# The first FFT of a Fourier filter and feed-forward kernel in four quadrants of 32 partitions

## The chip, the cores and the metric

The kernel runs on one core of one Trainium2 chip. The metric is the time of one execution on the device in microseconds. A core has TensorE (PE, with its weight loads shown apart as PEld), VectorE (DVE), ScalarE (ACT), GpSimd (POOL), SyncE (SP, which here only issues transfers) and 16 DMA engines. Operands lie in SBUF, and TensorE writes its results to PSUM.

## The reference

```
X = rfft(x, axis=1)                 # x: 8 x 3008 x 256, float32
y = irfft(X * (filt_r + 1j*filt_i)) # filters: 1505 x 256, one per frequency and channel
h = maximum(y @ w_in, 0)            # y as 24064 tokens of 256; w_in: 256 x 2048
out = (h * h) @ w_out               # w_out: 2048 x 256
```

All inputs and the output are float32 in HBM. Both kernels compute in float16 with float32 sums in PSUM.

## The kernel before

**The FFT.** A length of 3008 is split into 64 x 47, and each stage is a matmul with constant cosine and sine matrices. Stage A (`unit_a`, L333; for the first batch `chunk_a0`, L366) takes the 47-point transforms. Stage B (`unit_b`, L411) takes the 64-point transforms of each of 24 classes `c` of frequencies, multiplies with the filter on DVE (L425) and leaves the products in float16. A product has two versions `v`, one with the real and one with the imaginary part of the filter. Stage P (`unit_p0`, L438, for batch 0; `unit_p`, L455, for the others) is the inverse 64-point transform, evicted by ACT into `ze` (L450) and written to a DRAM scratch `dZ`. `read_z` (L476) reads it back in another order into `zt`, and stage Y (`unit_y`, L484) is the inverse 47-point transform, whose result `yt` is the input of the feed-forward part. Batches 1 to 7 go through DRAM between A and B as well (`write_u`, L326, `dU`, `read_u`, L404). Batch 0 stays on the chip there: its A gives the transposed `uT`, and `turn_u` (L388) turns it back by matmuls with the identity, evicted at L400 and L402.

**The filter.** B's products need it as `sF`: rows of both signs of a frequency on 128 partitions, by class. `load_f` (L234) loads it as float32 with 3008 numbers a partition, `tensor_copy` casts it, and `place_f` (L269) moves each row to its partition by matmuls with the 0/1 matrices `sPF` (L284 and L287, 108 in all), evicted with the sign of its half at L295. Stage P of batch 0 takes the imaginary version with `sSPx`, a copy of the constant `sSP` with its halves exchanged (L773, L774).

**The feed-forward part** works on 47 groups of 512 tokens, 8 slots a group (loop at L809). In each slot `ffn_g1` (L512) computes two tiles of 128 hidden units into one of two `psH` buffers (2 PSUM banks each) and ACT takes the relu into float16 (L532). DVE squares (`ffn_sq`, L534). One group later `products` (L632) computes the second matmul in seven products of sums of quarters, for which `make_t` (L586, slots 8 to 11) and `sums` (L602) prepare operands on DVE.

**The order of the work.** The prologue, about 50 us, is written out by hand from L735 on: `warm` matmuls (26, L264), the casts of x (`cast_wide`, L221), A, `turn_u`, `place_f`, then B of two class pairs, a placement and P in a loop, then `read_z`, A of batch 1, 13 `fill` matmuls (L798) and the first four Y units (L801). Then the slot loop runs, into which `fft_plan` (L669) places the stages of batches 1 to 7 and the rest of Y of batch 0 by due times in slots: for example, B of batch 1 from slot 12 on, Y(0, n) for n of 4 to 7 in slots 4 to 7, n of 8 to 11 in slots 10 to 13, with the zt for these read by `read_z(0, 2)`, the last line of the prologue. Each engine executes its instructions in the order of the program and waits where an operand or a buffer isn't ready. SP issues nearly all transfers, in its own order; POOL issues the float32-to-float16 loads `load_x` and `load_wout` (L320).

**Buffers.** [...] two `psH` tiles of two banks, `psF` and `psO` tiles. `bank_pair` hands the prologue these in turn.

Of the kernel before, what the change touches and what calls it, by code (L numbers as in the profile page):

```python
# [22 lines left out]
QF = 3008  # L23
PQ = ((0, 0), (0, 1), (0, 2), (1, 2), (1, 3), (1, 0))


def _build_consts():
# [28 lines left out]
    freq[0, 32] = N // 2  # L56
# [6 lines left out]
    for c in range(NC):  # L63
        for f in range(64):
# [10 lines left out]
            if c == 0 and f == 32:  # L75
                SB[:, :, 1, c, :, f] = 0.0
# [18 lines left out]
    PF = np.zeros((128, 6, 2, 2, 32))  # L95
    for w, (s, q) in enumerate(PQ):
        for j in range(32):
            PF[4 * j + q, w, :, s, j] = 1.0

# [7 lines left out]
    return f16(C0, 128), f16(PF, 128), f16(SB, 128), f16(SP, 128)  # L107
# [3 lines left out]
def kernel(  # L111
# [19 lines left out]
    C0_np, PF_np, SB_np, SP_np = _build_consts()  # L131
    dPF = nc.inline_tensor(PF_np, name="cPF")
# [13 lines left out]
    p_y = ctx.enter_context(tc.tile_pool(name="p_y", bufs=2))  # L146
# [58 lines left out]
    sPF = p_out.tile([128, 6, 128], F16, tag="ost", name="sPF")  # L205
# [3 lines left out]
    def load_wide(k):  # L209

        v0 = xrows[0:2048, :].rearrange("(p m) d -> p m d", m=16)
        v1 = xrows[2048:3072, :].rearrange("(p m) d -> p m d", m=8)
        pool, tag = (p_x32, "x32") if k < 2 else (p_h2, "h2")
        t = pool.tile([128, 8, D], F32, tag=tag, name=f"xw_{k}")
        nc.sync.dma_start(out=t, in_=(v0[:, 0:8, :], v1, v0[:, 8:16, :])[k])
        xw32[k] = t
# [4 lines left out]
    def cast_wide(k, *engs):  # L221
        t = p_x16.tile([128, 8, D], F16, tag="x16", name=f"xw16_{k}")
        for i in range(2):
            m = slice(4 * i, 4 * i + 4)
            cast(engs[i], t[:, m, :], xw32[k][:, m, :])
        xw16[k] = t

    for k in range(3):
        load_wide(k)


    f32s = []

    def load_f(im):  # L234
        filt = filt_i if im else filt_r
        t = p_y.tile([128, QF], F32, tag="yt", name=f"f32_{im}")
        nc.sync.dma_start(out=t, in_=filt[0:1504, :].rearrange("a d -> (a d)")
                          .rearrange("(p e) -> p e", e=QF))
        f32s.append(t)

    load_f(0)
    nc.sync.dma_start(out=sPF, in_=dPF.ap().rearrange("p (w q) -> p w q", q=128))
    load_f(1)
    nc.sync.dma_start(out=sC1, in_=dC0.ap()[:, 704:896])
    nyq = p_out.tile([128, 2, D], F32, tag="ost", name="nyq")
    nc.gpsimd.memset(nyq, 0.0)
    for im, filt in enumerate((filt_r, filt_i)):
        nc.gpsimd.dma_start(out=nyq[0:1, im, :], in_=filt[1504:1505, :])
    sSB = const.tile([128, NC, 128], F16, name="sSB")
    sSP = const.tile([128, NC, 128], F16, name="sSP")  # L250
    sign = const.tile([128, 1], F32, name="sign")
    nc.vector.memset(sign[0:64], 1.0)
    nc.vector.memset(sign[64:128], -1.0)


# [8 lines left out]
    for _ in range(26):  # L264
        nc.tensor.matmul(ps, zero, sF[:, 0, 0:2, :], start=True, stop=True)  # L265

    f16s = []

    def place_f(im, k, *engs, rotate=False):  # L269

        if rotate:
            banks, groups = bank_pair(f"psf_{im}_{k}")
        else:
            t = psH(f"psf_{im}_{k}")
            banks, groups = [t[:, 0, :], t[:, 1, :]], [(t, 0)]
        for i in range(4):
            c = 4 * k + i
            e0, e1 = D * c, D * (47 - c)
            cuts = [0] + [d for d in range(1, D)
                          if (e0 + d) % QF == 0 or (c and (e1 + d) % QF == 0)] + [D]  # L280
            for d0, d1 in zip(cuts, cuts[1:]):
                o = banks[i // 2][:, (i % 2) * D + d0:(i % 2) * D + d1]
                q, a = divmod(e0 + d0, QF)
                nc.tensor.matmul(o, sPF[:, PQ.index((0, q)), :], f16s[0][:, im, a:a + d1 - d0],  # L284
                                 start=True, stop=False)
                q, a = divmod(e1 + d0, QF) if c else (0, QF + d0)
                nc.tensor.matmul(o, sPF[:, PQ.index((1, q)), :], f16s[0][:, im, a:a + d1 - d0],  # L287
                                 start=False, stop=True)
        for t, i in groups:
            n = t.shape[1]  # L290
            eng = engs[i % len(engs)]
            dst = sF[:, im, 4 * k + 2 * i:4 * k + 2 * i + 2 * n, :]
            src = t.rearrange("p t (a d) -> p (t a) d", d=D)
            if eng is nc.scalar:
                eng.activation(out=dst, in_=src, func=AF.Copy, scale=sign[:, 0:1] if im else 1.0)  # L295
            elif im:
                eng.tensor_scalar_mul(out=dst, in0=src, scalar1=sign[:, 0:1])
            else:
                eng.tensor_copy(out=dst, in_=src)
# [4 lines left out]
    def load_win():  # L304

        for k, c, n, pool, tag in ((0, 0, 768, p_ze, "ze"), (0, 768, 768, p_ze, "ze"),
# [26 lines left out]
    def unit_a(b, c):  # L333
# [29 lines left out]
        if b == 1:  # L363
            write_u(b, c)

    def chunk_a0(c):  # L366

        for k in range(2):
            banks, groups = bank_pair(f"psA_0_{c}_{k}")
# [410 lines left out]
    for k in range(7):  # L780
# [5 lines left out]
        if k > 0:  # L786
            unit_p0(k - 1)
# [72 lines left out]
```

## Time and profile before

| | |
|---|---|
| median of 3 runs | 760.74 us (760.02 to 760.77) |
| the profiled execution | 757.66 us |
| its span, from first to last instruction | 755.9 us |
| TensorE clock granted | 1.00 |
| PE busy | 741.9 us, 98% |
| DVE busy | 655.4 us, 87% |
| ACT busy | 564.2 us, 75% |
| POOL busy | 193.9 us, 26% |
| HBM traffic | 57.97 MB read, 48.23 MB written, 141 GB/s over the span |

A line of the chain of waits gives start, length, engine, the name of the result, the line of the kernel and a count. A line of the groups gives line, engine, operation, result <- operands, shapes and count, then busy us and mean ns of one, then the engine's idle time ahead of the group with what ended it. The prologue in the trace: the first cast of x starts at 6.32 us, the first turn_u matmul at 17.80, the last `ze` copy of batch 0 ends at 42.26, the first Y matmul starts at 48.76, the first L528 matmul of the loop at 50.21.

### The profile page before, as it was taken

The numbers are of one execution on the slowest core, as the hardware profiler recorded it, in microseconds if no ns is written. First come the engines' busy times: TensorE is split into PE (matmuls) and PEld (weight loads), VectorE is DVE, ScalarE is ACT, GpSimd is POOL, SyncE is SP. The second block draws the span as 40 slices with busy tenths as digits, with TensorE's granted clock in tenths as the row PEclk, the third lists the DMA queues.
The fourth block names the chain that finished last, engine by engine and source line by source line (L and its number), as shares of the span: only waits on it lengthen the run. The fifth ranks groups of instructions, "written<-read, shape, count | busy, mean of one in ns | idle before, by whom it ended". The sixth has DMA issues, their size and how long they took to land.

```text
span 755.9 us, 20010 instructions
## 1 busy us (share of the span) xinstructions
PE 741.9 (98%) x8419; PEld 542.8 (72%) x8419; DVE 655.4 (87%) x730; ACT 564.2 (75%) x803; POOL 193.9 (26%) x267
## 2 busy tenths in 40 slices
PE   8988999999999999999999999999999999999998
PEld 5845766777777777877778777787678777777776
DVE  5859998899899898989979998899989989888783
ACT  2967788778878777787777778777777777777773
POOL 3811750244222321232303224033311222000000
PEclk9999999999999999999999999999999999999999
DMA  9994898666785566756586646764547333321011
GB/s 364 298 221 147 144 185 224 174 115 121 165 220 121 97 130 161 194 104 133 107 216 127 131 102 131 229 126 101 115 108 207 80 78 92 99 85 43 30 57 57
DMA packets 103026, 106.51 MB, mean 141 GB/s; under 512 B 10144, under 2 KB 93472, under 8 KB 101400
## 3 DMA queue, kind: packets, MB, share of 16 engines
q1 hardware_dynamic: 83496, 81.99, 35.7%
q0 software_dynamic: 19296, 23.05, 22.1%
q8 instruction: 66, 1.08, 0.6%
q14 instruction: 24, 0.20, 0.1%
q10 hardware_dynamic: 144, 0.18, 0.1%
HBM read 57.97 MB, written 48.23 MB: 141 GB/s over the span
## 4 chain that ended last, share of the span: by engine, by line
PE 90%; DVE 5%; ACT 2%; DMA 1%; issue 1%; ACTq 0%; DVEq 0%
PE psH L528 40%; PE psX L643 21%; PE psY L643 16%; PE psY L498 3%; PE psB L417 2%; PE psP L462 2%; PE psA L348 2%; DVE prod L425 2%; PE warm L265 1%; PE psO L548 1%; ACT h L532 1%; DVE h L539 1%; PE psf L284 1%; PE psf L287 1%; DMA prod<-prod 1%
## 5 line engine op out<-in xcount | busy, mean ns | idle before, releaser
L532 ACT ACTIVATE h<-psH 128x1024 f16<-128x1024 f32 x376 | 385.3, 1026 | 160.2 <-PE psH L528 159.2
L528 PE MATMUL psH<-yt,sWin 128*128 128x512 f16 (+7 forms) x1728 | 386.8, 351 | 1.2 <-ACT h L532 0.4
L539 DVE TENSOR_TENSOR h<-h 128x2048 f16<-128x2048 f16 (+1 forms) x192 | 229.8, 1197 | 45.5 <-ACT h L532 45.1
L432 POOL DMA_DIRECT2D prod<-prod x168 | 138.8, 967 | 428.5 <-DVE prod L425 426.1
L528 PEld LDWEIGHTS <-sWin 128*128 128x128 f16 x1728 | 149.1, 98 | 90.5 <-issue 3.0
L643 PEld LDWEIGHTS <-sum 128*128 128x128 f16 x2944 | 181.4, 98 | 26.2 <-issue 6.3
L643 PEld LDWEIGHTS <-h 128*128 128x128 f16 x2208 | 135.6, 98 | 24.5 <-issue 5.3
L425 DVE TENSOR_TENSOR prod<-psB,sF 128x1024 f16<-128x1024 f32 x84 | 102.3, 1219 | 11.9 <-PE psB L417 11.8
L643 PE MATMUL psX<-sT,sum 128*128 128x128 f16 x1472 | 104.7, 219 | 0.0
L643 PE MATMUL psY<-sT,sum 128*128 128x128 f16 x736 | 71.2, 219 | 0.0
L643 PE MATMUL psY<-sWout,sum 128*128 128x128 f16 x736 | 56.0, 219 | 1.4 <-DVE bot L658 1.4
L617 DVE TENSOR_TENSOR sum<-sum,h 128x2048 f16<-128x2048 f16 x46 | 56.1, 1220 | 0.8
L643 PE MATMUL psY<-sWout,h 128*128 128x128 f16 x736 | 56.2, 219 | 0.0
L643 PE MATMUL psX<-sT,h 128*128 128x128 f16 x736 | 56.1, 219 | 0.0
L620 DVE TENSOR_TENSOR sum<-h 128x2048 f16<-128x2048 f16 x46 | 56.0, 1217 | 0.0
L623 DVE TENSOR_TENSOR sum<-h,sum 128x2048 f16<-128x2048 f16 x46 | 55.9, 1216 | 0.0
L195 POOL DMA_DIRECT2D x<-in_x_dram x64 | 55.8, 1045 | 0.5 <-PE psA L348 0.5
L614 DVE TENSOR_TENSOR sum<-h 128x2048 f16<-128x2048 f16 x46 | 55.9, 1215 | 0.0
L464 ACT CAST ze<-psP 128x512 f16<-128x512 f32 x84 | 49.2, 585 | 1.2 <-PE psP L462 1.1
L643 PE MATMUL psX<-sWout,h 128*128 128x128 f16 x736 | 48.7, 219 | 0.0
L507 DVE CAST yt<-psY 128x376 f16<-128x376 f32 x62 | 33.7, 543 | 14.3 <-PE psY L498 14.1
L498 PE MATMUL psY<-sC,zt 112*128 112x94 f16 x512 | 42.3, 204 | 1.3 <-DMA zt<-dZ 0.9
(78 smaller groups left out, 571.3 us busy)
## 6 DMA issues: line engine op xcount, KB each, us to landing
zt<-dZ SPq DMA_DIRECT2D x64, 192.0 KB
dU<-u SPq DMA_DIRECT2D x56, 192.0 KB
prod<-prod POOLq DMA_DIRECT2D x168, 64.0 KB, 2.7
dZ<-ze SPq DMA_DIRECT2D x28, 384.0 KB
x<-in_x_dram POOLq DMA_DIRECT2D x48, 192.0 KB, 5.3
ut<-dU SPq DMA_DIRECT2D x7, 1024.0 KB
out_dram<-bot SPq DMA_DIRECT2D x32, 128.0 KB
out_dram<-top SPq DMA_DIRECT2D x16, 256.0 KB
```

What stands on the lines that cost most here:

```text
L195: nc.gpsimd.dma_start(out=t[64 * h + p0:64 * h + p1], in_=v[p0:p1, 8 * c:8 * c + 8, :])
L425: nc.vector.tensor_mul(out=prod, in0=ps.rearrange("p (a d) -> p a d", d=D).unsqueeze(1).to_broadcast([128, 2, 2, D]), in1=sF[:, :, 2 * p:2 ...
L432: nc.gpsimd.dma_start(out=prod[64 * i:64 * i + 64, 0], in_=prod[64 - 64 * i:128 - 64 * i, 1], accum_op=mybir.AluOpType.add)
L498: nc.tensor.matmul(ps[:, 94 * jj:94 * jj + 94], zt[:, 4 * (g % 2) + jj, dt * 128:(dt + 1) * 128], sSY, start=True, stop=True)
L528: nc.tensor.matmul(ps[:, i, o:o + n], sWin[:, dt, jt * 128:(jt + 1) * 128], yts[b][:, dt, r:r + n], start=(dt == 0), stop=(dt == 1))
L532: nc.scalar.activation(out=h2[:, 2 * s:2 * s + 2, :], in_=ps, func=AF.Relu)
L539: nc.vector.tensor_mul(out=v, in0=v, in1=v)
L614: nc.vector.tensor_add(out=t, in0=a21, in1=a22)
L617: nc.vector.tensor_sub(out=t, in0=f[5], in1=a11)
L620: nc.vector.tensor_sub(out=t, in0=a11, in1=a21)
L623: nc.vector.tensor_sub(out=t, in0=a12, in1=f[6])
L643: nc.tensor.matmul(o[:, t, :], f[p][:, q, 128 * t:128 * t + 128], sg["w"][p][:, q, :], start=(m == 0 and p in (1, 2)), stop=(q == 7), skip ...
```

## The change

The diff touches the first batch's FFT, the loading of the filter, and the order of the prologue. The stages of batches 1 to 7 and the feed-forward part keep their code.

- **x** comes in six halves of 4 KB rows, 512 KB each, in an order that gives the first two quarters of A their operands first. All six casts are on DVE, ahead of, between and behind A's evictions. 14 warm matmuls in place of 26.
- **The filter** is loaded once into `f32`, a float32 view of a buffer that later holds `yt`: four quadrants `q` of 32 partitions, 12 rows of 256 each, so that partition `32 q + j` holds rows `47 j + 12 q` and the eleven after it. `_cls(q, i)` is the class whose frequencies lie at row `i` of quadrant `q`. `place_f`, `sPF`, `nyq`, `sign` and the evictions are gone.
- **B of batch 0** (`unit_b0`) computes for one `i` all four quadrants: 8 matmuls with 128 rows and 32 output columns of the array, each to its quadrant of PSUM partitions. The product reads `f32` as it is and gives both versions of both parts.
- **P of batch 0** (`unit_p0`) takes each quadrant's 32 partitions as an array tile of 32 rows and 128 columns: 16 matmuls for one `i`, 4 for each of four classes, summed in PSUM over two `i` that share these classes (i and 11 - i). Its constants `sqs` are a rearranged SP in three versions. Both psH tiles are held for a pair; ACT copies one element after the first half of a pair (`junk`), and after the second the two `ze` halves, each with its own dZ transfer of 128 KB.
- **The filter for the other batches** still goes into `sF`: POOL casts it (`cast_f`), eight transfers from SBUF to SBUF on SP's queue (`spread_f`) after the first Y units bring it to the upper 64 partitions, and DVE writes the lower 64 in slots 9 to 12 (`mirror_f`).
- **Order.** `turn_u` of six class sets, B and P run interleaved as the loop over `m` shows. `load_wout` of both halves stands after `tiny`, a copy that waits for `zt`; `unit_a(1, 3)` moves behind the four Y units; 8 `fill` matmuls in place of 13; `sSP` is loaded at the end of the prologue, after the spread and ahead of `read_z(0, 2)`. B of batch 1 is due from slot 14 in steps of 15/11 of a slot instead of from 12 in steps of 16.5/11.

```diff
-QF = 3008
-PQ = ((0, 0), (0, 1), (0, 2), (1, 2), (1, 3), (1, 0))
+NS = 12
+WARM, FILL = 14, 8
+def _cls(q, i):
+    return (i, 12 + i, 23 - i, 11 - i)[q]
...
+    SQ = np.zeros((4, 32, 2, NS, 128))
+    for q in range(4):
+        for i in range(NS):
+            w = SP[:, 32 * (q // 2):32 * (q // 2) + 32, _cls(q, i)]
+            SQ[q, :, :, i] = w.reshape(2, 32, 128).transpose(1, 0, 2)
...
+    ybuf = const.tile([128, 2, 2 * NS * D], F16, name="ybuf")
+    f32 = ybuf.rearrange("p a b -> p (a b)").bitcast(F32).rearrange(
+        "p (v i d) -> p v i d", v=2, i=NS)
...
+        m = slice(4 * i, 4 * i + 4)
+        nc.sync.dma_start(out=xw32[k][:, m, :],
+                          in_=(v0[:, 0:8, :], v1, v0[:, 8:16, :])[k][:, m, :])
...
-    for k in range(3):
-        load_wide(k)
...
+    def cast_wide(k, i):
+        m = slice(4 * i, 4 * i + 4)
+        nc.vector.tensor_copy(out=xw16[k][:, m, :], in_=xw32[k][:, m, :])
+    HALVES = ((0, 0), (1, 0), (0, 1), (1, 1), (2, 0), (2, 1))
+    for k, i in HALVES:
+        load_wide(k, i)
+    def load_f(i0, i1):
+        for v, filt in enumerate((filt_r, filt_i)):
+            nc.sync.dma_start(
+                out=f32[:, v, i0:i1, :].rearrange("p i d -> p (i d)"),
+                in_=bass.AP(tensor=filt.tensor, offset=filt.offset + i0 * D,
+                            ap=[[12 * D, 4], [47 * D, 32], [1, (i1 - i0) * D]]))
...
+    def load_sb(c0, c1):
+        nc.sync.dma_start(
+            out=sSB.rearrange("p (h c) f -> p h c f", h=2)[:, :, c0:c1, :],
+            in_=dSB.ap().rearrange("p (h c f) -> p h c f", h=2, c=12)[:, :, c0:c1, :])
+    sqs = []
+    def load_sq():
+        for k in range(2):
+            t = p_u.tile([128, NS, 128], F16, tag="u", name=f"sq_{k}")
+            nc.sync.dma_start(out=t, in_=dSQ.ap().rearrange("p (k i b) -> p k i b", k=2, i=NS)[:, k])
+            sqs.append(t)
+        sqs.append(p_u.tile([128, NS, 128], F16, tag="u", name="sq_2"))
+    load_sb(3, 9)
+    load_f(3, 9)
+    load_sq()
+    load_sb(0, 3)
+    load_sb(9, 12)
+    load_f(0, 3)
+    load_f(9, 12)
+    nc.sync.dma_start(out=sC1, in_=dC0.ap()[:, 704:896])
...
-    for _ in range(26):
+    for _ in range(WARM):
         nc.tensor.matmul(ps, zero, sF[:, 0, 0:2, :], start=True, stop=True)
-    f16s = []
-    def place_f(im, k, *engs, rotate=False):
...
-                nc.tensor.matmul(o, sPF[:, PQ.index((0, q)), :], f16s[0][:, im, a:a + d1 - d0],
-                                 start=True, stop=False)
-                q, a = divmod(e1 + d0, QF) if c else (0, QF + d0)
-                nc.tensor.matmul(o, sPF[:, PQ.index((1, q)), :], f16s[0][:, im, a:a + d1 - d0],
-                                 start=False, stop=True)
...
-                eng.activation(out=dst, in_=src, func=AF.Copy, scale=sign[:, 0:1] if im else 1.0)
...
+    def unit_a0(c, k):
+        banks, groups = bank_pair(f"psA_0_{c}_{k}")
...
+    ORDER = (5, 4, 3, 2, 1, 0)
+    def turn_u(k, eng):
+        i = ORDER[k]
+        banks, groups = bank_pair(f"psT_{k}")
...
+        for j, c in enumerate((i, 11 - i)):
+            o = uts[0][:, c::12, :]
+            pv = banks[j].rearrange("p (h d) -> p h d", d=D)
...
+    def unit_b0(n):
+        i = (ORDER[n // 2], 11 - ORDER[n // 2])[n % 2]
+        if n % 4 > 1:
+            ps = psO(f"psB_0_{n}").rearrange("p a d -> p (a d)")
+        else:
+            ps = psF(f"psB_0_{n}")
+        for ri in range(2):
+            for q in range(4):
+                c, f = _cls(q, i), 64 * ri + 32 * (q // 2)
+                nc.tensor.matmul(ps[32 * q:32 * q + 32, ri * D:(ri + 1) * D],
+                                 sSB[:, c, f:f + 32], uts[0][:, c, :], start=True, stop=True)
+        if n == 0:
+            prods["ring"] = p_h2.tile([128, 6, 2, 2, D], F16, tag="h2", name="prods_0")
+        nc.vector.tensor_mul(
+            out=prods["ring"][:, n % 6],
+            in0=ps.rearrange("p (r d) -> p r d", d=D).unsqueeze(1).to_broadcast([128, 2, 2, D]),
+            in1=f32[:, :, i, :].unsqueeze(2).to_broadcast([128, 2, 2, D]))
+    pz = {}
+    junk = const.tile([128, 1], F32, name="junk")
+    def unit_p0(m):
+        k, n = divmod(m, 2)
+        if m == 0:
+            zes[0] = p_h2.tile([128, NC, D], F16, tag="h2", name="ze_0")
+        i = ORDER[k]
+        if n == 0:
+            pz["ts"] = [psH(f"psP_0_{k}_{j}") for j in range(2)]
+        ts = pz["ts"]
+        banks = {i: ts[0][:, 0, 0:D], 12 + i: ts[0][:, 1, 0:D],
+                 11 - i: ts[1][:, 0, 0:D], 23 - i: ts[1][:, 1, 0:D]}
+        j = (i, 11 - i)[n]
+        prod = prods["ring"][:, m % 6]
+        for t, (v, r, w) in enumerate(((0, 0, 0), (1, 0, 1), (0, 1, 1), (1, 1, 2))):
+            for q in range(4):
+                p = slice(32 * q, 32 * q + 32)
+                nc.tensor.matmul(banks[_cls(q, j)], sqs[w][p, j, :], prod[p, v, r, :],
+                                 start=(n == 0 and t == 0), stop=(t == 3),
+                                 skip_group_check=True)
+        if n == 0:
+            nc.scalar.copy(out=junk, in_=ts[1][:, 0, 0:1])
+            return
+        for c, t in ((i, ts[0]), (11 - i, ts[1])):
+            ze = zes[0][:, c::12, :]
+            nc.scalar.copy(out=ze, in_=t[:, :, 0:D])
+            nc.sync.dma_start(
+                out=dZ[0].rearrange("(s p) d -> p s d", p=128)[:, c::12, :], in_=ze)
...
+    f16s = {}
+    def cast_f(i0, i1):
+        for v in range(2):
+            if v not in f16s:
+                f16s[v] = p_x32.tile([128, NS, D], F16, tag="x32", name=f"f16_{v}")
+            nc.gpsimd.tensor_copy(out=f16s[v][:, i0:i1, :], in_=f32[:, v, i0:i1, :])
+    def spread_f(v):
+        for q in range(4):
+            o = sF[32 * (q // 2):32 * (q // 2) + 32, v]
+            o = (o[:, 0:12, :], o[:, 12:24, :], o[:, 23:11:-1, :], o[:, 11::-1, :])[q]
+            nc.sync.dma_start(out=o, in_=f16s[v][32 * q:32 * q + 32])
+    def mirror_f(k):
+        v, c = k % 2, slice(12 * (k // 2), 12 * (k // 2) + 12)
+        nc.vector.tensor_scalar_mul(out=sF[64:128, v, c, :], in0=sF[0:64, v, c, :],
+                                    scalar1=-1.0 if v else 1.0)
...
-                r = 12 + 16.5 * p / 11 if b == 1 else 6 + 28 * p / 11 if b == 2 else -2 + 36 * p / 11
+                r = 14 + 15 * p / 11 if b == 1 else 6 + 28 * p / 11 if b == 2 else -2 + 36 * p / 11
...
+    load_win()
+    for k, i in HALVES[:2]:
+        cast_wide(k, i)
+    unit_a0(0, 0)
+    unit_a0(2, 0)
+    for k, i in HALVES[2:4]:
+        cast_wide(k, i)
+    unit_a0(0, 1)
+    unit_a0(2, 1)
+    for i in range(2):
+        cast_wide(2, i)
+        unit_a0(1, i)
+        unit_a0(3, i)
+    nc.gpsimd.tensor_scalar_mul(out=sqs[2], in0=sqs[0], scalar1=-1.0)
+    cast_f(3, 9)
     for k in range(2):
-        c = slice(12 * k, 12 * k + 12)
-        load_const(sSB[:, c, :], dSB, k)
-        load_const(sSP[:, c, :], dSP, k)
-    load_win()
-    for c in (0, 2, 1, 3):
-        chunk_a0(c)
-    f16s.append(p_h2.tile([128, 2, QF + D], F16, tag="h2", name="f16"))
-    e0, e1 = slice(0, 1504), slice(1504, QF)
-    for im in range(2):
-        nc.gpsimd.tensor_copy(out=f16s[0][:, im, QF:], in_=nyq[:, im, :])
-    for e in (e0, e1):
-        nc.gpsimd.tensor_copy(out=f16s[0][:, 0, e], in_=f32s[0][:, e])
-    uts[0] = p_ut.tile([128, NC, D], F16, tag="ut", name="ut_0")
+        load_x(1, k)
...
+    cast_win()
     turn_u(0, nc.scalar)
     turn_u(1, nc.vector)
+    unit_b0(0)
+    unit_b0(1)
     turn_u(2, nc.scalar)
-    turn_u(3, nc.vector)
-    place_f(0, 0, nc.scalar, rotate=True)
-    for eng, e in ((nc.vector, slice(0, 1024)), (nc.gpsimd, slice(1024, 2048)),
-                   (nc.scalar, slice(2048, QF))):
-        cast(eng, f16s[0][:, 1, e], f32s[1][:, e])
-    turn_u(4, nc.vector)
-    place_f(0, 1, nc.scalar, rotate=True)
-    turn_u(5, nc.vector)
-    place_f(1, 0, nc.scalar, nc.vector, rotate=True)
-    for k in range(6):
-        if k % 3 == 0:
-            sSPx.append(p_u.tile([128, 12, 128], F16, tag="u", name=f"sSPx_{k}"))
-        c, o = slice(4 * k, 4 * k + 4), slice(4 * k % 12, 4 * k % 12 + 4)
-        nc.gpsimd.tensor_copy(out=sSPx[-1][0:64, o, :], in_=sSP[64:128, c, :])
-        nc.gpsimd.tensor_copy(out=sSPx[-1][64:128, o, :], in_=sSP[0:64, c, :])
-        if k < 4:
-            load_x(1, 2 * k)
-            load_x(1, 2 * k + 1)
-    load_wout(0)
-    cast_win()
-    for k in range(7):
-        if k < 6:
-            unit_b(0, 2 * k)
-            if k < 5:
-                place_f(1, k + 1, nc.scalar)
-            unit_b(0, 2 * k + 1)
-        if k > 0:
-            unit_p0(k - 1)
-        if k < 4:
-            place_f(0, k + 2, nc.scalar)
+    unit_b0(2)
+    turn_u(3, nc.scalar)
+    unit_b0(3)
+    turn_u(4, nc.scalar)
+    turn_u(5, nc.scalar)
+    for m in range(12):
+        unit_p0(m)
+        if m < 8:
+            unit_b0(m + 4)
...
-    load_wout(1)
-    for c in range(4):
+    for k in range(2):
+        load_wout(k)
+    for c in range(3):
...
-    for _ in range(13):
+    for _ in range(FILL):
...
+    unit_a(1, 3)
     prologue[0] = False
+    for v in range(2):
+        spread_f(v)
+    nc.sync.dma_start(out=sSP, in_=dSP.ap().rearrange("p (a b) -> p a b", b=128))
...
+        if 9 <= s < 13:
+            mirror_f(s - 9)
```

## The prediction

> **What bounds the kernel now.** I read the page first (busy shares, shares of the chain), then the chain in order of time for the first 66 us, then windows of 2 and 10 us, the groups of 17 to 43 us, and timelines of single engines.
>
> ```profile
> span 755.9 us, 20010 instructions
> PE 741.9 (98%) x8419; PEld 542.8 (72%) x8419; DVE 655.4 (87%) x730; ACT 564.2 (75%) x803; POOL 193.9 (26%) x267
> PE 90%; DVE 5%; ACT 2%; DMA 1%; issue 1%; ACTq 0%; DVEq 0%
> ```
>
> TensorE is busy 98% of the span and carries 90% of the chain. So the slot loop from 50 us on runs at TensorE's pace, and time lost ahead of it is not won back. The chain, by time, before the loop:
>
> ```profile
> 2.68 8.72 PE warm L265 x26
> 15.75 2.01 DVE uT L386 x4
> 17.80 1.90 PE psT L394 x31
> 38.21 2.36 DVE prods L425 x2
> 41.24 1.02 ACT ze L450
> 42.28 3.28 DMA dZ<-ze
> 45.58 3.04 DMA zt<-dZ
> 50.21 1.19 PE psH L528 x4
> ```
>
> The last ze copy ends at 42.26, dZ out and zt back take until 48.62, Y starts at 48.76, the loop at 50.21. Whatever moves 42.26 moves everything. Placing the filter (L284, L287) fills the chain from 19.7 on, with products and P between. Inside the loop the early slots have slack in one place only (start:end, length, busy PE, PEld, DVE, ACT, POOL, clock, DMA share, GB/s):
>
> ```profile
> 50.00:52.00 2.00, 1.79 (x8) 0.78 (x8) 0.52 (x1) 0.74 (x2) 0.00 (x0) 1.00 1.25 185
> 52.00:54.00 2.00, 1.75 (x9) 0.67 (x7) 0.61 (x1) 1.80 (x3) 0.00 (x0) 1.00 1.27 228
> 66.00:68.00 2.00, 2.00 (x26) 1.41 (x24) 2.00 (x4) 1.21 (x3) 0.00 (x0) 1.00 0.03 6
> 70.00:80.00 10.00, 8.21 (x92) 5.93 (x90) 10.00 (x13) 5.31 (x8) 5.87 (x8) 1.00 0.40 69
> ```
>
> From 50 to 58 the DMA engines are full (shares 1.25 and 1.27, then 1.16 and 1.11); from 66 they are empty; from 60 to 90 DVE has no gap.
>
> [...] The trace agrees for 64-wide tiles: L348's quads of four 512-column tiles start 0.23 us apart, where one such matmul alone takes 0.215, and a switch to or from them costs about 0.1 us. Tiles of 32 are not shown. [...] warm matmuls come 0.427 us apart up to 8.6 us, then 0.22. [...] The row of L425 below, 1218 ns for 1024 columns, agrees; float32 on the other side should cost the same.
>
> ```profile
> L425 DVE TENSOR_TENSOR prods<-psB,sF 128x1024 f16<-128x1024 f32 x12 | 13.9, 1218 | 2.2 <-ACT ze L450 1.9 <-issue 0.2
> L284 PE MATMUL psf<-f,sPF 128*128 128x256 f16 (+3 forms) x54 | 11.5, 260 | 0.3
> L450 ACT CAST ze<-psP 128x1024 f16<-128x1024 f32 x6 | 6.1, 1012 | 1.4 <-PE psP L448 1.4
> ```
>
> **Removed.** 108 placing matmuls (0.109 us apart: 11.8 us of TensorE), 13 evictions on ACT (6.6 + 6.2 us), 12 sSPx copies on POOL (2 x 3.7), half the filter casts. This empties the prologue between 19.7 and 38, but what sets its end then is the new order of waits.
>
> **Stage A.** x halves of 512 KB land 1.25 us apart (casts of before start at 6.32, 8.82 and 11.30, one 1 MB tile each). Fourteen warm matmuls end at 2.68 + 14 x 0.427 = 8.66, not 11.40. But all six casts are now on DVE, in one queue with its evictions: two casts, A, two evictions, two casts, and so on. A quarter of A is 16 matmuls, 0.72 us; a cast 0.65, an eviction of 384 columns 0.50. So: A to 10.1; evictions to 11.3, casts to 12.6; A to 14.1; cast 14.8 to 15.5; A to 17.0; evictions to 18.15, cast to 18.85; A to 20.35; evictions to 21.05. T starts at 21.1 instead of 17.8: +3.3.
>
> **T, B and the products.** T's two first units 21.1 to 22.0; ACT's eviction gives B(0) at 22.9 and the first product at 23.5 (1.2 us each, 1.16 apart). T2 and T3 wait for PSUM banks that the products hold, T4 and T5 after them; ACT's four half evictions for T4 and T5 end at 31.2. P(0) needs both psH buffers, which these hold: it starts at 31.25. B(4) stands behind it on TensorE, so DVE idles from 29.7 to 32.7.
>
> **P.** Each pair of classes holds both psH buffers until both its copies are done, so nothing overlaps: P(2k), 16 matmuls as four rounds of four tiles, four starts 0.109 apart and 0.27 for the last, 0.67; the 1-element ACT copy 0.2 with 0.09 of hand-over; P(2k+1) 0.67; two copies of 512 columns, 1.09 as a pair (the trace's 585 ns alone[...]), with 0.08 of hand-over. Sum 2.8; the two products, 2.32, fit in it. Bounds: 2.7 if copies overlap[...]. Six pairs: 31.25 + 16.8 = 48.1, against 42.26: **+5.9** (+5.1 to +9.4).
>
> **dZ and zt.** The last dZ is half as large but every zt read must now wait for it; before, the first pair was read at 43.20. I take 5.95 against 6.5, so Y is at +5.3. unit_a(1,3) stands between Y and the loop: 8 tiles and its waits for banks, 1.1 us. Loop at **+6.4**.
>
> **SP's queue.** After the eight dU writes SP now issues eight spread copies of the filter (1.57 MB), sSP (0.79 MB), and only then zt of tokens 1504 on. Both sWout loads also start later, after zt; each took 8.9 us to land before, the earlier of them under the prologue. At 421 GB/s (1 MB of x in 2.49 us) the first two are 5.6 us, sWout's two 1 MB halves (float32) 5, so some 11 us of full queues go into a stretch already at 1.1 to 1.3. SP also has to issue nine more transfers first, at 0.8 (zt, two in 1.57) to 1.0 us (dU, eight in 8.04): 7 to 9 us, partly while the queues work. Zt(0,2) then lands some 19 us after the loop starts. Its Y unit stands at slot 10, about 14.5 us in; TensorE runs into it and waits. Waiting 0 (all goes past it) to 9; I take **+3.5**, since make_t and the sums can't fill it: they are on DVE. The first sums also wait for the spread, whose float16 sources hold their buffers; that comes due before zt, so I add nothing for it. On POOL, batch 1's x loads now stand behind the filter casts, but A(1) comes about 5 us later: nothing.
>
> **mirror.** Four tensor_scalar of 64 x 3072 f16, slots 9 to 12, where DVE has no gap. No row shows this operation; [...] DVE leads TensorE only partly there, and the stall covers some: 0 to 6.6, I take **+1**. B(1) is due from slot 14, not 12: same work, nothing.
>
> **Sum.** 6.4 + 3.5 + 1 = 10.9. On the profiled execution's 757.66 (span 755.9 and 1.8 around it) 768.6. The median of the runs shown, 760.74, lies 3.1 above that execution; on it, 771.6.
>
> **Rivals.**
> - *Transfers stay hidden.* The empty queues of 66 to 74 us speak for it (share 0.03), the full ones ahead of them against. 6.4 and a bit of mirror: 767.5. Chance 0.22.
> - *Transfers worse.* The 512-byte rows of half of the spread make them slow, stall 9: 777. Chance 0.07.
> - *Clock falls back.* With A waiting on DVE and P busy less than half the time, TensorE may be granted half. Then each start in P is 0.109 later, 8 a pair, 0.87 x 6 = 5.2: 776.8. [...] Chance 0.13.
> - *The tiles don't overlap.* Then P is 16 starts, 1.31 us more each, 12 times 15.7, and B 8 starts instead of 2: 787 to 789. The change wouldn't do what it says. Against: L348's overlap. Chance 0.08.
> - *Faster.* If P's copies hand back buffers early enough, the prologue runs at its twelve products: 23.5 + 12 x 1.16 = 37.4, the tail 2.7, end 40.1, 2.15 ahead; -0.6 + 1.1 and hidden transfers leave -1.65: 759.1. This decides below a period of about 1.5 us a pair if T ends as I say, or if T isn't held up by the banks at 2.0. The row of L425 speaks for it (DVE alone is 13.9 us long), the double hold of psH against. Chance 0.08, of which 0.05 are under 759.2.
>
> Mine keeps 0.42. A measurement of this kernel can't tell less than about 0.2%, 1.5 us, from no change. Faster 0.06, same 0.03, slower 0.91. The range, 762 to 785, leaves out the faster case and the tiles that don't overlap, and takes in a stall of 0 to 9 and periods of 2.7 to 3.45.
>
> **What would show it.** T's first matmul near 21.1; P(0) near 31.2; ze's pairs 2.8 us apart, the last ending near 48.1; Y near 54; the loop's first L528 near 56.6; a TensorE wait on zt, slot 10, of some us; mirror rows of 0.96; clock 1.00. I am wrong if casts don't queue behind evictions, if the pair's period is near 2, or if zt lands by slot 10.

## The result, and the profile after

The changed kernel takes 800.47 us (median of 4 runs, 797.04 to 801.15), the kernel before 760.38 (4 runs): a ratio of 1.0521, 95% interval 1.0488 to 1.0555. That is 40 us slower, where 11 were forecast and the range ended at 785. (Two statements above need setting right: `spread_f` writes partitions 0 to 63 of `sF`, `mirror_f` 64 to 127; and in the kernel before the first `turn_u` matmul starts at 17.36 us, not at 17.80.)

The page of the changed kernel, with the busy shares, the granted clock and the DMA engines' share in 40 slices, and the chain by engine:

```profile
span 795.2 us, 20213 instructions
PE 751.9 (95%) x8510; PEld 540.4 (68%) x8510; DVE 656.0 (83%) x728; ACT 556.0 (70%) x808; POOL 189.2 (24%) x253
PEclk8655889999999999999999999999999999999999
DMA  8278958975767645784658655684546433431111
PE 81%; DMA 5%; DVE 3%; issue 1%; ACT 1%; POOL 0%; SPq 0%; DVEq 0%
```

The loss is all in the first six slices of 20 us: there the clock is at half for most of the time (0.68 in the mean up to relu 11, where the kernel before has 1.00), and in the second slice the DMA engines, which the kernel before kept full, are at 0.2. From relu 32 of 376 on, the distance between the two kernels hardly moves (38.7 us; 39.2 at the last relu). Along the way, in us from the start (relu 0 is the loop's first, and relu 11 is the first behind the Y unit that needs the second pair of `zt`):

| | before | changed | e1 | e4 | e10 |
|---|---|---|---|---|---|
| first `turn_u` matmul | 17.36 | 21.99 | 22.30 | 16.55 | 17.23 |
| first product of batch 0 | 24.62 | 32.72 | 26.04 | 21.36 | 21.96 |
| first P matmul | 26.77 | 40.86 | 34.05 | 29.38 | 29.79 |
| last `ze` copy of batch 0 ends | 42.25 | 65.42 | 57.04 | 51.54 | 48.54 |
| first Y matmul of batch 0 | 48.76 | 76.02 | 63.31 | 57.81 | 56.63 |
| relu 0 | 51.41 | 81.64 | 67.39 | 61.81 | 61.12 |
| relu 10 | 63.35 | 94.51 | 79.50 | 73.93 | 73.33 |
| relu 11 | 65.16 | 105.08 | 93.42 | 87.71 | 86.65 |

DVE's timeline in the changed kernel (start, length, engine, line, operation, in brackets the idle time before and what ended it) has two waits that the prediction doesn't know:

```profile
23.77 1.29 DVE L384 CAST ut<-psT 128x512 f16<-128x512 f32 x2 [1.11 <-PE psT L377]
32.72 2.36 DVE L407 TENSOR_TENSOR prods<-psB,ybuf 128x1024 f16<-128x1024 f32 x2 [7.66 <-DMA ybuf<-in_filt_r_dram]
...
54.87 5.75 DVE L407 TENSOR_TENSOR prods<-psB,ybuf 128x1024 f16<-128x1024 f32 x5 [6.39 <-DMA ybuf<-in_filt_i_dram]
```

Both are waits for the filter. It isn't that the queues are full meanwhile; they are mostly empty. Windows of the changed kernel (start:end, length, busy PE, PEld, DVE, ACT, POOL, clock, DMA share, GB/s):

```profile
8.00:12.00 4.00, 1.90 (x39) 1.63 (x37) 2.22 (x4) 0.86 (x2) 0.00 (x0) 1.00 1.02 410
20.00:32.00 12.00, 4.20 (x58) 3.41 (x57) 2.40 (x4) 2.03 (x4) 0.00 (x0) 0.78 0.30 110
```

While x loads, the engines move 410 GB/s; while the filter loads, 110, with 0.30 of them busy. Further on, the chain in order of time:

```profile
68.77 2.80 DMA dZ<-ze
...
72.17 3.71 DMA zt<-dZ
...
83.45 8.57 DMA sF<-f
92.02 0.02 issue
92.04 9.43 DMA zt<-dZ
101.47 0.14 issue
101.60 0.47 PE psY L524 x4
```

The chain puts the wait of the Y unit at slot 10 down to the spread and then to the second pair of `zt`: relu 11 comes 10.57 us after relu 10, where it was 1.81 before.

### The profile page after: what moved, and what is told of

Read it like the earlier page. It is cut to its first block, busy times and chain, and to the rows that moved or that the text cites. A ratio compares the mean times of both kernels' runs of the same rounds, so it can differ in the third digit from the quotient of the medians.

```text
span 795.2 us, 20213 instructions
## 1 busy us (share of the span) xinstructions
PE 751.9 (95%) x8510; PEld 540.4 (68%) x8510; DVE 656.0 (83%) x728; ACT 556.0 (70%) x808; POOL 189.2 (24%) x253
## 3 DMA queue, kind: packets, MB, share of 16 engines
q0 software_dynamic: 19232, 23.05, 20.9%
## 4 chain that ended last, share of the span: by engine, by line
PE 81%; DMA 5%; DVE 3%; issue 1%; ACT 1%; POOL 0%; SPq 0%; DVEq 0%
PE psH L554 37%; PE psX L669 19%; PE psY L669 15%; PE psY L524 3%; PE psP L488 2%; PE psB L446 2%; PE psA L329 2%; DMA prod<-prod 2%; DMA zt<-dZ 2%; DVE h L565 1%; DMA sF<-f 1%; DVE prod L449 1%; PE psO L574 1%; DMA dZ<-ze 0%; DVE sum L649 0%
## 5 line engine op out<-in xcount | busy, mean ns | idle before, releaser
L554 PE MATMUL psH<-ybuf,sWin 128*128 128x512 f16 (+7 forms) x1728 | 389.3, 353 | 0.7 <-ACT h L558 0.2
L533 DVE CAST ybuf<-psY 128x376 f16<-128x376 f32 x62 | 33.6, 542 | 23.0 <-PE psY L524 14.9
L524 PEld LDWEIGHTS <-zt 112*128 112x128 f16 x512 | 33.7, 99 | 25.4 <-DMA zt<-dZ 7.6
```

Source lines behind the costliest of these rows:

```text
L524: nc.tensor.matmul(ps[:, 94 * jj:94 * jj + 94], zt[:, 4 * (g % 2) + jj, dt * 128:(dt + 1) * 128], sSY, start=True, stop=True)
L554: nc.tensor.matmul(ps[:, i, o:o + n], sWin[:, dt, jt * 128:(jt + 1) * 128], yts[b][:, dt, r:r + n], start=(dt == 0), stop=(dt == 1))
```

## The experiments

Three suspects followed from this: the way the filter is loaded, the order of stage A, and the transfers at the start of the loop; TensorE's clock was the fourth. Times are medians; each is set against the runs of the kernel before that were made with it (758.96 us for e1 to e4, 758.56 for e5 to e8, 760.09 for e9 to e12), and "over before" is that difference. The changed kernel is 40.1 over before.

**e1: the filter by quadrants.**

```diff
-            nc.sync.dma_start(
-                out=f32[:, v, i0:i1, :].rearrange("p i d -> p (i d)"),
-                in_=bass.AP(tensor=filt.tensor, offset=filt.offset + i0 * D,
-                            ap=[[12 * D, 4], [47 * D, 32], [1, (i1 - i0) * D]]))
+            for q in range(4):
+                nc.sync.dma_start(
+                    out=f32[32 * q:32 * q + 32, v, i0:i1, :].rearrange("p i d -> p (i d)"),
+                    in_=bass.AP(tensor=filt.tensor, offset=filt.offset + (12 * q + i0) * D,
+                                ap=[[47 * D, 32], [1, (i1 - i0) * D]]))
```

> Only edit: each load of the filter is issued as four transfers, one per quadrant, whose outermost dimension counts 32 rows instead of 4. Theory [...] (0.2 to 0.3 of the engines busy and about 105 GB/s from 19 to 38 us). Then the first half lands by 17 to 19 us, the first product starts near 25 us instead of 32.7, DVE's wait of 6.4 us for the filter's second part (to 54.9) is gone, and the first relu of the loop is at 62 to 68 us instead of 81.6: 778 to 786 us in all. Rival 'order and volume': the filter is late because it stands in one queue with everything else; then the first product stays near 32 us and the time at 797 to 801.

786.11 us, 27.2 over before: 13 less than the changed kernel. The same bytes now come with the engines busy where they were mostly idle, and DVE has no wait for the filter left; the products follow the casts at once. Windows and DVE's timeline of e1:

```profile
20.00:24.00 4.00, 3.56 (x41) 3.24 (x39) 1.12 (x2) 0.97 (x3) 0.81 (x1) 0.50 1.01 321
```

```profile
24.84 1.29 DVE L385 CAST ut<-psT 128x512 f16<-128x512 f32 x2 [1.88 <-PE psT L378]
26.04 2.35 DVE L408 TENSOR_TENSOR prods<-psB,ybuf 128x1024 f16<-128x1024 f32 x2
```

321 GB/s where it was 110, and a share of 1.01 where it was 0.30. So the form in which the load is issued sets its pace here. That the outermost count does it was my estimate: e1 raises the count from 4 to 32 and also makes four transfers of each one, and the trace doesn't name the engine of a packet. A whole transfer isn't slow as such: those of x, 512 KB each, move at 410 GB/s.

**e2: zt ahead of the spread.**

```diff
+    read_z(0, 2)
     for v in range(2):
         spread_f(v)
     nc.sync.dma_start(out=sSP, in_=dSP.ap().rearrange("p (a b) -> p a b", b=128))
-    read_z(0, 2)
```

> Only edit in the changed kernel: zt of the tokens from 1504 on is read before the eight spread transfers and sSP, not after. Theory: these stand ahead of it in SP's queue and make TensorE wait 7.1 us, and ACT's relu 11 lose 8.8 us; then zt lands by 90 us instead of 101.5, the wait is gone and the time falls by 6 to 9 us, to 789 to 794. Rival: the queues are full whatever the order, and the spread, now later, holds up the mirror, the sums (whose buffers its sources hold) and B of batch 1: the wait moves there and the time falls by 0 to 3 us.

797.92 us, 39.0 over before, about that of the changed kernel. The rival has it: the Y unit comes at 94.36 instead of 101.60, but the first sum, whose buffer the spread's sources hold, now waits, and the mirrors come after it on a DVE that has no gap left. DVE in e2:

```profile
92.59 0.68 DVE L621 TENSOR_TENSOR sT<-sWout 128x1024 f16<-128x1024 f16 x1
95.52 1.23 DVE L640 TENSOR_TENSOR sum<-h 128x2048 f16<-128x2048 f16 x1 [2.24 <-DMA sF<-f]
```

By relu 16 e2 is 37.6 behind the kernel before, the changed kernel 37.5. Moving this `zt` forward only moves the wait.

**e3: fillers ahead of A and P**, on e1: the first call stands in `unit_a0`, the second in `unit_p0`.

```diff
+    def keep(o, n):
+        for _ in range(n):
+            nc.tensor.matmul(o, zero, sF[:, 0, 0, 0:o.shape[-1]], start=True, stop=True,
+                             skip_group_check=True)
...
+        keep(banks[0][:, 0:256], 10)
...
+        keep(ts[0][:, 0, D:2 * D], 6)
```

> e1 and, ahead of each quarter of stage A, 10 matmuls of 256 columns with zeros, and 6 ahead of each P unit, into PSUM that is overwritten or not read. They compute nothing. Theory: TensorE's clock falls to half because A and P leave it idle, and it stays there; with the gaps filled the clock is 1.00 from 6 to 50 us, P's pairs come 2.8 to 3.2 us apart instead of 3.7, and the time is 4 to 8 us under e1. Rival: with the filter in time the clock doesn't fall, or P's pace is set by waits between engines; then the fillers only cost their own time: 1 to 8 us over e1.

787.16 us, 1 over e1, within the spread of these runs (785.82 to 788.51): inconclusive. (The output of e3 is off by 0.15. Ahead of the second unit of a pair the fillers write into a bank that holds one of P's unfinished sums; that this is the cause was not shown.) The clock stayed at 1.00 until 29.5 us (0.985 in the mean of the run, 0.962 in e1), but the fillers held up the stage that they were to speed: `turn_u` starts at 24.47, 2.2 later than in e1.

**e4: stage A in the order of before, with its 26 warm matmuls**, on e1.

```diff
-WARM, FILL = 14, 8
+WARM, FILL = 26, 8
...
+    for k, i in HALVES:
+        cast_wide(k, i)
+    for c, i in ((0, 0), (2, 0), (0, 1), (2, 1), (1, 0), (3, 0), (1, 1), (3, 1)):
+        unit_a0(c, i)
```

> e1 and the order of stage A of the kernel before: all six casts on DVE ahead of every eviction, and 26 warm matmuls. Theory: the casts between the evictions make A run 3 to 4 us longer; then the first turn_u matmul is near 17.8 us instead of 22.0, TensorE isn't idle in A, the clock stays full through A and T, and the time is 3 to 7 us under e1. Rival: the filter or the PSUM banks bound the products then, and the start of T doesn't matter: within 1 us of e1.

780.57 us, 21.6 over before and 5.5 under e1, as the theory has it. `turn_u` starts at 16.55, the first product 3.3 us earlier than even in the kernel before. Yet relu 11 is 22.5 us later than before, and 12 of these come between relu 10 and 11.

**e5: spread and sSP within P; e6: the first half of sWout as before; e7: both, and the ze copies on two engines**, all on e4.

```diff
     for m in range(12):
         unit_p0(m)
         if m < 8:
             unit_b0(m + 4)
+        if m in (6, 7):
+            spread_f(m - 6)
+        if m == 8:
+            nc.sync.dma_start(out=sSP, in_=dSP.ap().rearrange("p (a b) -> p a b", b=128))
```

> e4 with the eight spread transfers and sSP issued between P units 6 and 8, where the queues have room (0.22 to 0.25 of them busy from 52 to 60 us in e1), not after the first Y units. Theory: it is the volume in the first 25 us of the loop, not its order, that makes zt late (e2 moved the order and the wait went to the sums, behind the spread's landing); without the spread and sSP there, relu 11 follows relu 10 within 4 us instead of 13.8, and the time is 8 to 11 us under e4, 769 to 773. Rival: dU and sWout alone fill the queues there: 0 to 4 us under e4.

```diff
+    load_wout(0)
     cast_win()
...
-    for k in range(2):
-        load_wout(k)
+    load_wout(1)
```

> e4 with the first half of sWout loaded where the kernel before loads it, ahead of the casts of w_in on POOL, not after zt. Theory: of the transfers in the loop's first 25 us this is the smaller part (1 MB of float32 against 1.6 and 0.8 MB): 1 to 4 us under e4. Rival: sWout is what blocks (it takes 10.5 us to land there): 6 to 11 us under e4, and e5 gains little.

```diff
-            nc.scalar.copy(out=ze, in_=t[:, :, 0:D])
+            cast(nc.scalar if c == i else nc.vector, ze, t[:, :, 0:D])
```

> e5 and e6 together, and of the two ze copies of a pair one on ACT and one on DVE instead of both on ACT. Theory: the wait in the loop is gone and the two copies, 1.07 us on the cycle of a pair that can't overlap with anything, become 0.6: the pairs of P come 3.2 us apart instead of 3.73, the loop starts 2.5 to 3 us earlier than in e4, and the time is 764 to 769. Rival: with half the clock TensorE and the products set the pace, and a copy on DVE delays the products: the period stays at 3.6 or more, 769 to 773.

787.13, 780.57 and 788.95 us: 28.6, 22.0 and 30.4 over before, none under e4's 21.6. In e5 the wait at slot 10 is gone (relu 11 comes 1.8 us after relu 10), as its theory says, but the last dZ now stands in SP's queue behind half of the spread (L474) and sSP (L795). e5's chain, in which SPq is SP issuing transfers:

```profile
53.36 0.10 SPq L441
...
53.55 0.56 SPq L474
...
56.29 0.98 SPq L795
...
59.82 4.86 DMA dZ<-ze
...
65.11 3.69 DMA zt<-dZ
...
68.93 0.47 PE psY L525 x4
```

15.6 us from the last `ze` copy to Y, where e4 takes 6.3: the last dZ is issued 6.5 us after its copy, and its transfer takes 4.9. In e7 it is issued 10.2 us after its copy. So the order in SP's queue can cost much. In e6 the loop starts 4.0 us later than in e4 and relu 11 comes 0.7 earlier. In e7 the last pairs of P come 2.4 to 2.9 us apart (the clock is 1.00 there), and Y still starts at 69.83. Each move is paid back elsewhere; both the theories and the rivals of e5 and e6 were wrong about the total. This led to a theory on the DMA share of the whole stretch up to relu 11. Windows of the kernel before, of e4, e6 and e9, one fence each:

```profile
0.00:65.16 65.16, 58.28 (x553) 39.18 (x554) 44.49 (x55) 43.40 (x58) 25.70 (x43) 1.00 0.98 295
```

```profile
0.00:87.71 87.71, 64.14 (x655) 34.14 (x656) 47.98 (x55) 35.02 (x64) 21.07 (x29) 0.75 0.97 245
```

```profile
0.00:87.04 87.04, 66.95 (x655) 34.87 (x656) 47.93 (x55) 35.14 (x64) 21.06 (x29) 0.74 0.98 247
```

```profile
0.00:81.18 81.18, 64.24 (x655) 33.38 (x656) 49.35 (x52) 34.97 (x63) 31.07 (x31) 0.78 0.92 245
```

Length times share is the time of all packets, divided by 16 engines; I call it transfer work. It is 64 us before and 85 in e4 and e6 (87 in e1, 83 in the changed kernel), close to the length of the window in the kernel before, e4 and e6. The theory: up to slot 11 the transfers are the bound, although most of the chain of waits is TensorE's.

The windows alone don't show that. Packets of one engine overlap in this measure (the share is 1.31 in e4 from 64 to 68 us), so that a mean near 1 doesn't mean full engines throughout: in e4 it is 0.60 and 0.73 in the two stretches of 4 us from 24 to 32 us, and 0.43 and 0.58 from 48 to 56. Nor are the bytes the bound: e4 moves 21.5 MB in its window, and e11 (below) 21.7 MB in one that is 15 us shorter. So the theory needs runs that add or remove transfers.

**e8: fillers in P's waits**, on e4, behind `unit_b0(m + 4)`.

```diff
+        for _ in range(5 if m % 2 else 2):
+            nc.tensor.matmul(pz["ts"][1][:, 1, D:2 * D], zero, sF[:, 0, 0, :], start=False,
+                             stop=True, skip_group_check=True)
```

> e4 and matmuls of 256 columns with zeros in the waits of P, 2 after the first and 5 after the second unit of a pair, into columns that nothing reads. They compute nothing. Theory: P is on half clock because its waits leave TensorE too little work; filled, the clock rises to 1.00 within P and the period of a pair falls from 3.73 to 2.8 to 3.1: 3 to 5 us under e4. Rival: the clock doesn't answer to such work, or the period is set by the chain of waits and not by the clock: the same as e4 or up to 5 us over it.

784.08 us, 25.5 over before. The clock is 1.00 from 34.9 us to the end of P (0.983 in the mean of the run, 0.971 in e4), but the pairs stay 3.78 us apart: the five fillers didn't run in the wait but behind the copies that it waits for (TensorE idles 0.84 us ahead of them), and 0.65 us of each pair is their own. The rival's number, but not its reason.

**e9: no spread, no mirror; e10: fillers that wait for nothing; e12: longer rows**, on e4; **e11: the kernel before with more traffic.**

```diff
+    nc.gpsimd.memset(sF[:, 0, 2:, :], 0.0)
+    nc.gpsimd.memset(sF[:, 1], 0.0)
...
-    for v in range(2):
-        spread_f(v)
...
-        if 9 <= s < 13:
-            mirror_f(s - 9)
```

> e4 without the eight spread transfers and without the mirror (sF is set to zero, so that batches 1 to 7 are computed with a filter of zeros). Theory 'sum of the transfers': up to relu 11 the time is that of the DMA engines, 64.2 of 65.2 us in the kernel before, 84.9 of 87.7 in e4, whatever the order; the spread is some 8 us of it. Then relu 11 starts at 78 to 81 us and the time is 6 to 9 us under e4. Rival: the wait comes from zt's own latency, dU and sWout; without the spread it stays, 0 to 3 us under e4.

773.75 us, 13.7 over before: 7.9 under e4. The transfer work up to relu 11 is 75 us (its window stands above) and relu 11 at 81.18. TensorE's wait for `zt` in e4 and in e9:

```profile
84.00 0.47 PE L525 MATMUL psY<-sC,zt 112*128 112x94 f16 x4 [10.11 <-DMA zt<-dZ]
```

```profile
78.24 0.33 PE L527 MATMUL psY<-sC,zt 112*128 112x94 f16 x4 [3.28 <-DMA zt<-dZ]
```

Without the spread and the mirror there is some 10 us less transfer work, and the wait is 6.8 us shorter. This isn't the price of the traffic alone, because SP also has eight transfers fewer to issue ahead of this `zt`. SP's timeline in e4 and in e9:

```profile
63.29 9.10 SPq L474 DMA_DIRECT2D sF<-f  x8
...
73.33 2.15 SPq L507 DMA_DIRECT2D zt<-dZ  x2
```

```profile
67.43 1.14 SPq L509 DMA_DIRECT2D zt<-dZ  x2
```

In e9 `zt` is issued 5.9 us earlier, and from there to the Y unit it takes 10.8 us, in e4 10.7: the earlier issue accounts for all of the earlier Y. Whether SP itself is slow or waits for transfers ahead (2.8 us of its time at the spread are waits for dU) isn't separated, nor is the mirror's part. For e10, in `unit_b0` ahead of its matmuls:

```diff
+        for _ in range(6 if n >= 4 and n % 2 else 0):
+            nc.tensor.matmul(ps[:, 0:D], zero, sF[:, 0, 0, :], start=True, stop=True)
```

> e4 and 6 matmuls of 256 columns with zeros ahead of every second B unit of the loop with P, into that unit's own bank, which it then overwrites. They compute nothing and, unlike e8's, wait for no copy of ze. Theory: e8's fillers stood behind the ze copies and cost what the clock gave (3.78 less 0.65 and 0.3 is 2.85); here the clock is 1.00 in P from the second pair on, and the pairs come 2.8 to 3.1 us apart instead of 3.73. The time falls by less, 0 to 4 us, where the transfers are the bound. Rival: the clock isn't what makes P slow: 3.6 to 4.0 us apart.

ACT's timeline, two pairs in e4 and two in e10:

```profile
36.74 1.07 ACT L440 CAST ze<-psP 128x512 f16<-128x512 f32 x2 [1.32 <-PE psP L432]
...
40.47 1.08 ACT L440 CAST ze<-psP 128x512 f16<-128x512 f32 x2 [1.31 <-PE psP L432]
```

```profile
39.36 1.07 ACT L442 CAST ze<-psP 128x512 f16<-128x512 f32 x2 [0.72 <-PE psP L434]
...
42.06 1.07 ACT L442 CAST ze<-psP 128x512 f16<-128x512 f32 x2 [0.72 <-PE psP L434]
```

The same copies, 3.73 us apart at half clock and 2.70 at full: the clock costs 1.03 a pair, and it is bought back with work that computes nothing. P ends 3.0 us earlier than in e4, but Y starts only 1.2 earlier, because dZ and `zt` take 8.1 us in between instead of 6.3; relu 11 comes 1.1 earlier. The time is 781.00 us, 20.9 over before against e4's 21.6, which these runs don't tell apart. That fits a bound by the transfers and doesn't show it. For e11, in the kernel before:

```diff
     load_win()
+    spare = dram.tile([128, 3 * NC * 128], F16, name="spare")
+    for k in range(3):
+        nc.sync.dma_start(out=spare[:, NC * 128 * k:NC * 128 * k + NC * 128], in_=dSP.ap())
```

> The kernel before and three copies of a constant of 0.79 MB from HBM to HBM, which nothing waits for, issued on SP's queue behind the loads of w_in. Theory 'sum of the transfers': the DMA engines are full up to relu 11 (64.2 of 65.2 us), so 6 to 10 us more of their work make the kernel 5 to 10 us slower. Rival: the kernel before is bound by TensorE there, as the chain of waits has it, and the queues have room: 0 to 2 us slower.

765.81 us against 760.09: ratio 1.0077, interval 1.0047 to 1.0107. In the profile the first ten relus come 7.29 us later, and the window up to relu 11 has a share of 0.98 again:

```profile
0.00:72.45 72.45, 59.93 (x553) 40.00 (x554) 44.86 (x55) 43.84 (x58) 25.70 (x43) 0.95 0.98 299
```

71 us of transfer work, 7 more, for 7.3 us. No instruction waits for these copies, and SP has issued them by 27 us, ahead of its first dZ at 28.66; they only use the engines. This is the one run that changes traffic and nothing else. (In the longer wait for `zt` TensorE's clock fell too, to 0.95 in the mean.) For e12, where the load of x is issued for i of 0 only:

```diff
-        m = slice(4 * i, 4 * i + 4)
-        nc.sync.dma_start(out=xw32[k][:, m, :],
-                          in_=(v0[:, 0:8, :], v1, v0[:, 8:16, :])[k][:, m, :])
+            nc.sync.dma_start(out=xw32[k], in_=(v0[:, 0:8, :], v1, v0[:, 8:16, :])[k])
...
-            nc.gpsimd.tensor_copy(out=f16s[v][:, i0:i1, :], in_=f32[:, v, i0:i1, :])
+            nc.gpsimd.tensor_copy(out=f16s[v][0:64, i0:i1, :], in_=f32[0:64, v, i0:i1, :])
+            nc.gpsimd.tensor_copy(out=f16s[v][64:128, 12 - i1:12 - i0, :][:, ::-1, :],
+                                  in_=f32[64:128, v, i0:i1, :])
...
-            o = (o[:, 0:12, :], o[:, 12:24, :], o[:, 23:11:-1, :], o[:, 11::-1, :])[q]
+            o = (o[:, 0:12, :], o[:, 12:24, :], o[:, 12:24, :], o[:, 0:12, :])[q]
```

> e4 with x in three loads of 8 KB rows instead of six of 4 KB, and with the filter cast in reversed class order for the upper two quadrants, so that all eight spread transfers have rows of 6 KB instead of half of them 512 bytes. POOL has 6 us more to cast. Theory: x of 3.15 MB took 9.9 us of the DMA engines in 4 KB packets and 7.6 in 8 KB, 0.79 MB in 512 bytes some 5 and in 6 KB some 3: 4 us less transfer work, 3 to 5 us under e4. Rival: the number of bytes counts and not the rows' length: within 1 us of e4.

781.04 us, 21.0 over before: within 1 us of e4, the rival. The transfer work up to relu 11 (by the packets' own times) is 84.0 us against 84.9. Making these rows longer hardly shortens it.

None of these kernels beats the kernel before.

## Why the prediction was wrong

The direction was right, the size wrong by a factor of 3.7.

**The step that failed: "T, B and the products".** It let the first product start at 23.5 us, when B's result is there, and never asked when the filter is. Its load was priced nowhere: 421 GB/s was measured on x, and every other transfer was taken to move like x. It moved at 110 GB/s: the first product came at 32.72, and a second wait of 6.39 us followed within P, of which P lost some 1.5: one pair of its copies comes 5.28 us after the pair before, where the others come 3.55 to 3.74 apart. e1 gives the price of this step, 13 us of the 40. The shape of the transfer stood in the diff. (The products themselves were right: with the float32 filter one takes 1224 ns, against 1218 before.)

**Stage A** was right in its reasoning (casts queued behind evictions, `turn_u` late: measured 21.99 against a forecast of 21.1). Its size was low: against the true 17.36 of the kernel before the delay is 4.6 us, not 3.3. The stage ran at half clock from 12.5 us on, which the forecast left out. e4 takes 5.5 us off, but it restores the order and the warm matmuls at once, and their parts aren't told apart.

**P**: the chain of a pair was right to 0.1 us. It said 2.8 at full clock and 0.87 more at half; e10 has 2.70 and the changed kernel 3.73, while filter waits don't break in. (Its 0.67 for a unit doesn't follow from its parts: three gaps of 0.109 and the last 0.27 make 0.60. Its bounds of 2.7 and 3.45 a pair come out at +5.2 and +9.7; the 3.45 was an estimate of mine, and no run shows it. Nothing rests on either.) The tiles of 32 do overlap in fours: 16 of their matmuls take 1.04 us at half clock in the changed kernel (from 43.35 us), and at full clock ACT waits 0.72 for them in e10, where one after the other they would take 3.49 and 1.74 by the 0.109 of one at full clock. What failed was the choice between the two: the rival "clock falls back" got 0.13, because I took a long gap to be needed, which no trace had shown. The clock fell at 12.5 us with no gap longer than 1.72; in the window of 8 to 12 us above, TensorE is busy for 1.90 of 4 us, where the kernel before has 4.00 and kept 1.00. And it stayed at half while P kept TensorE busy for 7.53 of 8 us by the profile, in which the ends of matmuls are modelled (36 to 44 us in e4). In the kernel before, TensorE is busy for 9.89 and 9.42 us of the two stretches of 10 us from 20 to 40, at a clock of 1.00, with the placing matmuls among its work; their removal I had booked as pure gain.

**dZ and zt** took 10.6 us from the last `ze` copy to Y, not 5.95; in e1 and e4, 6.3. From there to relu 0 it took 5.62 us instead of 2.65: 3.0 more, where 1.1 were forecast for `unit_a(1, 3)` at full clock.

**SP's queue**: mechanism half right, size wrong. A wait at slot 10 came: TensorE waits 7.13 us and relu 11 loses 8.8 (12 in e1 and e4), where 3.5 were taken from a bound of 0 to 9. The Y unit came due 14.8 us after the loop's start, as forecast (14.5); `zt` landed 21.8 us after it, not 19. Moving that `zt` forward is no cure (e2), but SP's order and its issuing count (e5, e7, e9). Traffic counts too, and it was priced at its bytes over 421 GB/s: in e11 2.36 MB cost 7.3 us up to relu 11, where that price gives 5.6. In the prediction I looked at the DMA share from 50 us on only; in the 50 us before, the kernel before has 0.97. "Time lost ahead of the loop is not won back" is true; "whatever moves 42.26 moves everything" isn't the whole: added transfers move it as well. Of the 21 us of transfer work that e4 has over the kernel before, the spread's are 10; the rest (x in halves, the filter in 3 and 6 KB rows, the 0.79 MB of `sqs`) wasn't taken apart, and e12 shows only that longer rows don't recover it.

**What stays open.** e1 and e4 explain some 18.5 of the 40 us. In e4 21.6 are left. It is 22.5 us late at relu 11; by the table 10.4 of these are there at relu 0 (9.3 of them at the last `ze` copy), and 12 arise at the wait for `zt`. How much of that wait is traffic and how much SP's issuing, no run here separates.

**mirror**: 0.95 us each, forecast 0.96; that and the 6.6 of its range were estimates that no trace had shown. Its part in the end wasn't separated from the spread's.

**The rivals**: "transfers worse" and "clock falls back", each priced alone at 777, both happened, together with a wait that no rival named. Of the first only the stall is confirmed, not its reason: without the 512-byte rows nothing is gained (e12, 21.0 us over before against e4's 21.6). "Faster" had nothing for it: even with P at 2.70 and T at 17.2 (e10) P ends 6.3 us later than in the kernel before, and the kernel is 21 us slower.

## What to carry to other kernels

Ask of every new transfer at what rate one of its form has moved, before asking how many bytes it has: loads of the same rows moved at 110 GB/s as one transfer with an outermost count of 4 and at 321 as four with 32. Ask next what stands ahead of it in the queue that issues it: eight issues of the spread took 9.1 us of SP's time in e4, and half of them ahead of the last dZ, together with sSP, held it up by 6.5 us in e5. A transfer moved out of one wait can land in another, so compare the total and not the wait. And work that looks superfluous may be what holds TensorE's clock: in e10 six matmuls with zeros a pair held it at 1.00 in P, where e4 has 0.50 and 1.03 us more a pair. Before removing such work, count how busy the stage is without it.

## What was unexpected of the hardware

- Two loads of 768 KB in rows of 6 KB: 0.30 of the DMA engines and 110 GB/s as one transfer each with an outermost count of 4 (20 to 32 us of the changed kernel), 321 GB/s at a share of 1.01 as four transfers of 32 rows each (20 to 24 us of e1).
- The clock fell to half without a gap of more than 1.72 us (the changed kernel, at 12.5 us), and didn't rise in 8 us in which TensorE was busy 94% of the time by the profile's modelled ends (e4, 36 to 44 us); with some 0.65 us more matmuls a pair it held 1.00 (e10, 36 to 48 us).
- 2.36 MB copied from HBM to HBM, which nothing waits for, cost 5.7 us (interval of the ratio 1.0047 to 1.0107).
